# Pooled sums of the first batch on TensorE, loads of the second batch on SyncE, constants and masks later

## The chip, the cores and the metric

One core of one Trainium2 chip. The metric is the device time of one execution of the program in microseconds (us); every time below is in us from the start of the profiled span unless it says otherwise.

## The reference, cut to what matters

Inputs are q, k, v of 4 batches, 8 heads, 576 positions and 64 numbers a head, and the weights of two mixtures of experts. The first stage adds two attentions: one over queries, keys and values pooled by fours, and one over the neighbours less than four positions away.

```
q_d, k_d, v_d = (x.reshape(B, H, Sd, 4, D).mean(axis=3) for x in (q, k, v))
out_up = np.repeat(sm_attn(q_d, k_d, v_d), 4, axis=2)
out_local = softmax(where(|i - j| < 4, scale * q @ k.T, -1e9)) @ v
x = out_up + out_local                        # 2304 tokens of 512
x = x + gate * relu(x @ w1[e]) @ w2[e]        # best of 8 experts, where x @ w_skip > 0
out = sum over the two best of 8 experts of weight * relu(x @ u1[e]) @ u2[e]
```

All of it is computed in fp32 or in splits that keep its precision.

## The kernel before, in words

**Stages.** From about 1 to 130 us the attention runs, with the routing of the first mixture beside its second half; then come the experts of the first mixture and, from some 300 us on, those of the second.

**Units and pushes.** The attention is a list of units. `Local(t)` is one of 18 tiles of 128 tokens (four windows of 32), `Pooled(b, u)` is one of five parts of the pooled attention of batch b. `push(unit)` (from line 1104) writes out one step of a software pipeline: the scores of this unit (PE, then the maximum and the subtraction on DVE), the transposes (`turn`) of the unit two pushes back (`D1`), a list of fills that other code has asked for with `schedule(n, f)` (f runs n pushes later), the exponential (ACT), and `values` of the unit three pushes back (`D2`). PE, ACT, DVE and POOL keep this written order; SP's order is the planner's, which places a transfer when it expects it to be ready. In this text push n is the n-th call, from 0: pushes 0 to 3 are tiles 0 to 3, 4 to 6 are P(0,4), P(0,0), P(0,1), 7 is tile 4, 8 and 9 are P(0,2), P(0,3), 10 is tile 5, 11 to 13 are P(1,4), P(1,0), P(1,1), 14 is tile 6, 15 and 16 are P(1,2), P(1,3), 17 is tile 7; the pooled units of batch 2 begin with push 20.

**Sums of four.** A pooled unit of batch b needs qd (queries summed by fours) and kd (keys in two halves, [:, :, 0] and [:, :, 1]). For batch 0 all are reductions on DVE (`tensor_reduce`, four of qd, four of each half of kd; lines 776 and 786). For batch 1 all are additions on POOL: three for kd[:, :, 0] and three for qd (line 759), three for kd[:, :, 1] (line 789), in this order, from push 7 on. For batch 2 the queries are summed on POOL (`pool_q`, push 10). `pool_v(b, 0)` and `pool_v(b, 1)` sum the values by fours with matmuls (lines 798 and 805) and copy them out on ACT; the second then asks for the values of the next batch (`load_v`), into the same buffer. They run at push 3 for batch 0, push 7 for batch 1, push 14 for batch 2.

**Loads.** `load_qk(b)` (line 752) loads queries into qT (1152 KB) and the two halves of the keys into kT (576 KB each). For batch 1 the queries are issued by POOL, the first half of the keys by SP and the second by ACT. `load_local(t)` (line 890) loads the values of the windows of tile t in two halves of 192 KB, one issued by SP and one by ACT. An issue is an instruction in its engine's order: while it waits, what is written behind it waits too.

**POOL's order around the change.** Clears of buffers and index patterns (pushes 0 and 1), a small store to x_d, the queries of batch 1, `routing_constants` (lines 160 to 188, called by `start_3` at push 2), the four loads of `load_wall` (line 1182, at push 3), then the sums of batch 1. The masks that `start_3` asks for are two DVE operations each (lines 709 and 710). `load_wall` also asks for a copy into `wall` on DVE 12 pushes later (line 1183), which `x_part` uses. `finish(t)` schedules for each tile the addition of the pooled part (`x_add`, POOL, line 1006), its transposes on PE one push later (`x_turn`, line 1012) and the logits.

**Start.** 20 warm matmuls on zeros (`WARM`, line 621) run on PE while the first queries and keys arrive.

Of the kernel before, what the change touches and what calls it, by code (L numbers as in the profile page):

```python
# [10 lines left out]
F32 = mybir.dt.float32  # L11
# [3 lines left out]
AF = mybir.ActivationFunctionType  # L15
OP = mybir.AluOpType
# [8 lines left out]
NPOOL = S // 4  # L25
# [13 lines left out]
CH = ((0, 384), (384, 640))  # L39
EARLY = CH[0][1] // BLK2  # L40
MAGIC = 12582912.0
WARM = 20
FILL = 0
FILLS = {2: 2}
BUSY = {"turn15": 1, "table": 2, "turn16": 3, "part16": 1, "end": 3}
# [32 lines left out]
D2 = 3  # L78
NEP = 3
EPS = 48  # L80
ONDVE = (0,)
ONPOOLQ, ONPOOLQD, QDP, WALLP = (1,), (2,), 0, 12
NVG = 1
XB = 8
UB = 4
LOADQK = (-1, -1, 5, 9)
POOLQK = (2, 4, 6, 10)
POOLV = (3, 4, 6, 10)
QKS = 4
VS = 0  # L90
PATTERN = ((4, 0, 1), (2, 3))
POOLED = (3, 5, 9, 12)

# [10 lines left out]
def moe_attention_kernel(ctx, tc, q, k, v, w_skip, w_gate, w1, w2, g2, n2, noise, u1, u2, out, dbg=None):  # L104
# [507 lines left out]
    with ExitStack() as actx:  # L612
# [124 lines left out]
            load_qk(1)  # L737

        def start_3():
            routing_constants()  # L740
            for d in offsets:
                mask(d)


        fours = at.tile([128, 32], F32, name="fours", bufs=1)
# [2 lines left out]
        def load_qk(b):  # L748

            held["k", b % 2] = b  # L750
            qT[b] = at.tile([128, 4, S], F32, name="qT", bufs=2)
            (nc.gpsimd if b == 1 else nc.sync).dma_start(qT[b], q[b])
            for g in range(2):
                (nc.sync, nc.scalar)[g].dma_start(kTs[b % 2][g:128:2, g], k[b, 64 * g:64 * g + 64])

        def pooled_on_gpsimd(o, x):
            x = x.rearrange("p a (g r) -> p a g r", r=4)
# [7 lines left out]
        def pool_qk(b, n):  # L765


            assert held["k", b % 2] == b
            held["kd", b % 2] = (b, n)
            if n == 0 and b not in ONPOOLQD:  # L770
                qd[b] = at.tile([128, 4, NPOOL], F32, name="qd", bufs=2)
            kd, kT = kds[b % 2], kTs[b % 2]
            if n >= 8 and b in ONDVE:
                for i in range(n - 8, 4, 3):
                    o, x = kd[:, i, 1], kT[:, 1, i]
                    nc.vector.tensor_reduce(o, x.rearrange("p (g r) -> p g r", r=4), axis=AX.X, op=OP.add)
            elif b in ONPOOLQ and n < 8:
                if n == 0:
                    pooled_on_gpsimd(kd[:, :, 0], kT[:, 0])
                    pooled_on_gpsimd(qd[b], qT[b])  # L780
            elif n % 2 == 0 and n < 8 and b in ONPOOLQD:
                pass
            elif n < 8:
                i = n // 2
                o, x = (qd[b][:, i], qT[b][:, i]) if n % 2 == 0 else (kd[:, i, 0], kT[:, 0, i])
                nc.vector.tensor_reduce(o, x.rearrange("p (g r) -> p g r", r=4), axis=AX.X, op=OP.add)
            else:
                o, x = kd[:, :, 1], kT[:, 1].rearrange("p a (g r) -> p a g r", r=4)
                nc.gpsimd.tensor_tensor(o, x[:, :, :, 0] if n == 8 else o, x[:, :, :, n - 7], op=OP.add)
# [378 lines left out]
        pooled_keys(0)  # L1168
        pooled_keys(1)
        vgs[0] = load_v(0, A)  # L1170

        nc.vector.tensor_scalar(before, jp, 0.0, None, op0=OP.is_gt)
        nc.vector.memset(onesb, 1.0)
# [15 lines left out]
        for t in range(NT):  # L1189
            for b in range(B):  # L1190
                if LOADQK[b] == t:
                    load_qk(b)
                    if b in ONPOOLQD:
                        schedule(QDP, pool_q, b)
                if POOLQK[b] == t:
                    for n in range(8):
                        schedule(n // QKS, pool_qk, b, n)
                    for n in range(3):
                        schedule(n // 2 if b in ONDVE else n, pool_qk, b, n + 8)
                if b == 0 and t == EXP4 and UPE:  # L1200
                    schedule(0, expansion)
                if POOLV[b] == t:
                    schedule(0, pool_v, b, 0)
                    schedule(VS, pool_v, b, 1)
            if t == 3:
                load_wall()
            if t < 3:
                schedule(0, lambda: None)
# [762 lines left out]
```

## Time and profile before

| what | value |
| --- | --- |
| median of 3 runs (lowest to highest) | 780.25 us (778.61 to 781.01) |
| the profiled execution's own time | 780.45 us |
| its span, first to last instruction | 778.5 us |
| busy time of PE / DVE / ACT / POOL in the span | 755.6 / 351.3 / 249.6 / 255.0 us |
| mean granted clock of TensorE | 0.989 |

PE is TensorE's matmuls, PEld its weight loads, DVE VectorE, ACT ScalarE, POOL GpSimd, SP SyncE; a q behind an engine's name marks its issuing queue. [...] Matmuls are pipelined and their ends are modelled, so starts are surer than durations. An fp32 matmul is recorded as two passes. "idle before" names what ended the idle time of an engine; where the engine named had long been done, it was another, often a transfer.

### The profile page before, as it was taken

Reading aid. Unit: us, or ns where it says so; the run is one execution under the profiler, and the core shown is the slowest. Engines: PE = TensorE matmul, PEld = TensorE weight load, DVE = VectorE, ACT = ScalarE, POOL = GpSimd, SP = SyncE. Lnnn points to the kernel's source line nnn. Section 1 sums busy time; section 2 is a strip of 40 time slices with the busy share of each in tenths; the row PEclk is TensorE's granted clock in tenths of the full one; section 3 lists DMA queues with packets and bytes.
Section 4 is the critical chain, followed back from the end, with each engine's and each line's share of the span. In section 5 each row is a group of like instructions: output and inputs, shape, how many; then the busy total and the mean of one; then the engine's idle time right before and its main releaser. Section 6 shows DMA issues by size and latency. Waiting matters only on the chain.

```text
span 778.5 us, 15158 instructions
## 1 busy us (share of the span) xinstructions
PE 755.6 (97%) x6215; PEld 664.3 (85%) x6215; DVE 351.3 (45%) x805; ACT 249.6 (32%) x492; POOL 255.0 (33%) x257
## 2 busy tenths in 40 slices
PE   6999998999999999999999999999999999999996
PEld 3567785999999999989998998998998997997984
DVE  8776877510111755469854343262242343342200
ACT  3444553111112133224334343233233242333211
POOL 8782422211232351133364205215115115002012
PEclk9899999999999999999999999999999999999998
DMA  8988578699988872331556626526436336333013
GB/s 287 301 263 272 156 187 283 183 371 355 314 313 259 307 282 97 103 69 43 144 170 172 180 82 166 112 87 174 105 106 159 80 110 159 87 84 67 8 16 46
DMA packets 61128, 131.51 MB, mean 169 GB/s; under 512 B 15585, under 2 KB 16928, under 8 KB 59520
## 3 DMA queue, kind: packets, MB, share of 16 engines
q1 hardware_dynamic: 31552, 56.64, 23.4%
q10 hardware_dynamic: 17248, 46.66, 16.6%
q0 software_dynamic: 12256, 27.21, 16.6%
q8 instruction: 50, 0.82, 0.4%
q14 instruction: 22, 0.18, 0.1%
HBM read 101.86 MB, written 23.91 MB: 162 GB/s over the span
## 4 chain that ended last, share of the span: by engine, by line
PE 76%; issue 2%; DVE 1%; DMA 1%; POOL 0%; ACT 0%; POOLq 0%; DVEq 0%; ACTq 0%
PE pY L1612 27%; PE pH L1595 26%; PE pH L560 9%; PE pY L573 9%; PE pT L1580 2%; PE pT L592 1%; PE pT L539 1%; DMA rows<-x_d,ix2g 1%; PE pT L346 1%; PE pH L581 0%; POOL out L317 0%; DVE w L337 0%; PE pH L597 0%; PE pT L223 0%; DVE hl L1600 0%
## 5 line engine op out<-in xcount | busy, mean ns | idle before, releaser
L1612 PE MATMUL pY<-w,hh 128*128 128x512 f32 (+6 forms) x640 | 201.5, 396 | 0.0
L1595 PE MATMUL pH<-xh,w 128*128 128x256 f32 (+7 forms) x1024 | 196.0, 303 | 0.0
L1595 PEld LDWEIGHTS pH<-xh,w 128*128 128x128 f32 x1024 | 162.9, 188 | 0.8
L1612 PEld LDWEIGHTS pY<-w,hh 128*128 128x128 f32 (+6 forms) x640 | 115.0, 183 | 27.6
L1271 DVE TENSOR_TENSOR w<-stg,w 128x1024 fp32r<-128x1024 f32 x64 | 82.5, 1298 | 108.1 <-ACT w L1270 108.0
L1612 PE MATMUL pY<-w,hl 128*128 128x512 f32 (+6 forms) x320 | 125.6, 393 | 0.0
L1595 PE MATMUL pH<-xl,w 128*128 128x256 f32 (+7 forms) x512 | 123.5, 302 | 0.0
L1600 DVE SCALAR_TENSOR_TENSOR hl<-pH,hh 128x256 fp32r<-128x256 f32 (+7 forms) x128 | 57.0, 474 | 128.8 <-ACT hh L1599 128.5
L317 POOL DMA_INDIRECT out<-yo,ix2w x35 | 68.8, 1967 | 130.0 <-ACT yo L1614 121.5
L1599 ACT ACTIVATE hh<-pH 128x256 fp32r<-128x256 f32 (+7 forms) x128 | 49.3, 424 | 151.8 <-PE pH L1595 151.6
L1595 PEld LDWEIGHTS pH<-xl,w 128*128 128x128 f32 x512 | 90.1, 188 | 0.0
L312 POOL DMA_INDIRECT rows<-x_d,ix2g x32 | 36.2, 1132 | 155.4 <-PE pT L1580 144.2
L1612 PEld LDWEIGHTS pY<-w,hl 128*128 128x128 f32 (+6 forms) x320 | 58.5, 183 | 15.3
L573 PE MATMUL pY<-hT,w 128*128 128x112 f32 (+7 forms) x512 | 69.2, 296 | 0.0
L1270 ACT ACTIVATE w<-stg 128x1024 fp32r<-128x1024 f32 x64 | 66.8, 1054 | 6.8 <-DMA stg<-in_moe_w 6.8
L1614 ACT ACTIVATE yo<-pY,gt 128x512 f32<-128x512 f32 (+6 forms) x35 | 24.1, 688 | 138.3 <-PE pY L1612 77.4
L573 PEld LDWEIGHTS pY<-hT,w 128*128 128x128 f32 x512 | 67.4, 190 | 0.2
L560 PE MATMUL pH<-xT,w 128*128 128x200 f32 (+6 forms) x448 | 66.2, 301 | 0.0
L560 PEld LDWEIGHTS pH<-xT,w 128*128 128x128 f32 x448 | 61.1, 190 | 1.8 <-issue 1.7
L317 POOL DMA_INDIRECT l_d<-x,ix1w x15 | 14.3, 953 | 87.9 <-DVE x L600 87.0
L575 DVE COPY yT<-pY 128x224 f32<-128x224 f32 (+7 forms) x16 | 7.5, 471 | 73.8 <-PE pY L573 73.8
L1006 POOL TENSOR_TENSOR x<-x,up 128x512 f32<-128x512 f32 x15 | 19.3, 1291 | 42.5 <-DMA up<-od 32.6
(426 smaller groups left out, 851.4 us busy)
## 6 DMA issues: line engine op xcount, KB each, us to landing
w<-in_moe_w ACTq DMA_DIRECT2D x16, 2048.0 KB, 12.5
stg<-in_moe_w SPq DMA_DIRECT2D x64, 512.0 KB, 3.6
x_d<-x SPq DMA_DIRECT2D x18, 264.0 KB, 4.1
out<-zero ACTq DMA_DIRECT2D x3, 1536.0 KB, 7.6
up<-od SPq DMA_DIRECT2D x14, 256.0 KB, 5.1
qT<-in_q SPq DMA_DIRECT2D x3, 1152.0 KB, 5.5
vw<-in_v SPq DMA_DIRECT2D x18, 192.0 KB, 5.5
vw<-in_v ACTq DMA_DIRECT2D x18, 192.0 KB, 5.5
```

Of the source, the lines that this page charges most:

```text
L312: return nc.gpsimd.indirect_dma_start(out=dst, out_offset=None, in_=x_d[0:n + 1], in_offset=bass.IndirectOffsetOnAxis(ap=idx, axis=0))
L317: return nc.gpsimd.indirect_dma_start(out=dst, out_offset=bass.IndirectOffsetOnAxis(ap=idx, axis=0), in_=src, in_offset=None, **kw)
L560: nc.tensor.matmul(self.p[:, j], w[:, k, f * 128:(f + 1) * 128], self.xT[:, k], start=k == 0, stop=k == KD - 1)
L573: nc.tensor.matmul(p[:, j], w[:, f, d * 128:(d + 1) * 128], self.hT[:, f], start=f == 0, stop=f == KF - 1)
L1006: e.tensor_tensor(xs[t][:, 0:DM], xs[t][:, 0:DM], ups[t], op=OP.add)
L1270: nc.scalar.activation(hi[:, c], st[i], AF.Copy)
L1271: V.tensor_tensor(lo[:, c], st[i], hi[:, c].bitcast(F32), op=OP.subtract)
L1595: nc.tensor.matmul(p, w[:, k, fs], self.x[ch][n][:, k, 0:ch[1] - ch[0]], start=k == 0 and i == 0, stop=k == KD - 1 and i == 2)
L1599: nc.scalar.activation(hi, p, AF.Relu)
L1600: V.scalar_tensor_tensor(lo, p, 0.0, hi.bitcast(F32), op0=OP.max, op1=OP.subtract)
L1612: nc.tensor.matmul(p, h[:, f], w[:, f], start=f == 0 and i == 0, stop=f == KF - 1 and i == 2)
L1614: nc.scalar.activation(o, p, AF.Copy, scale=gate[0:n])
```

## The change

`ONDVE` becomes `ONPE`: for batch 0, qd and kd[:, :, 1] are summed by matmuls of the identity with every fourth column, four of them added up in PSUM for each of two tiles, and copied out by ACT; qd ahead of the first push, kd[:, :, 1] at pushes 2 and 3. kd[:, :, 0] of batch 0 stays on DVE. `WARM` goes from 20 to 14. The queries and both halves of the keys of batch 1 are issued by SP. The masks move from push 2 to push 5 and the constants to push 10. `pool_v` moves from push 3 to 5 (batch 0), from 7 to 11 (batch 1) and from 14 to 15 (batch 2); batch 3 stays. `load_wall` moves from push 3 to push 10 and its copy from push 15 to 16.

```
-WARM = 20
+WARM = 14
...
-ONDVE = (0,)
-ONPOOLQ, ONPOOLQD, QDP, WALLP = (1,), (2,), 0, 12
+ONPE = (0,)
+ONPOOLQ, ONPOOLQD, QDP, WALLT, WALLP = (1,), (2,), 0, 5, 6
...
-POOLV = (3, 4, 6, 10)
+POOLV = (3, 5, 6, 10)
 QKS = 4
-VS = 0
+VD = (2, 1, 1, 0)
...
         def start_3():
-            routing_constants()
-            for d in offsets:
-                mask(d)
+            schedule(7, routing_constants)
+            schedule(2, lambda: [mask(d) for d in offsets])
...
-            (nc.gpsimd if b == 1 else nc.sync).dma_start(qT[b], q[b])
+            nc.sync.dma_start(qT[b], q[b])
             for g in range(2):
-                (nc.sync, nc.scalar)[g].dma_start(kTs[b % 2][g:128:2, g], k[b, 64 * g:64 * g + 64])
+                (nc.sync, nc.sync if b == 1 else nc.scalar)[g].dma_start(kTs[b % 2][g:128:2, g], k[b, 64 * g:64 * g + 64])
+
+        def pooled_on_pe(o, x):
+            p = bank("pB", [128, 2, NPOOL])
+            x = x.rearrange("p a (g r) -> p a g r", r=4)
+            for i in range(2):
+                for j in range(4):
+                    nc.tensor.matmul(p[:, i], ident, x[:, i, :, j], start=j == 0, stop=j == 3)
+            nc.scalar.activation(o, p, AF.Copy)
...
-            if n == 0 and b not in ONPOOLQD:
+            if n == 0 and b not in ONPOOLQD + ONPE:
...
-            if n >= 8 and b in ONDVE:
-                for i in range(n - 8, 4, 3):
-                    o, x = kd[:, i, 1], kT[:, 1, i]
-                    nc.vector.tensor_reduce(o, x.rearrange("p (g r) -> p g r", r=4), axis=AX.X, op=OP.add)
+            if n >= 8 and b in ONPE:
+                if n != 9:
+                    pooled_on_pe(kd[:, n - 8:n - 6, 1], kT[:, 1, n - 8:n - 6])
...
-            elif n % 2 == 0 and n < 8 and b in ONPOOLQD:
+            elif n % 2 == 0 and n < 8 and b in ONPOOLQD + ONPE:
                 pass
...
         vgs[0] = load_v(0, A)
+        qd[0] = at.tile([128, 4, NPOOL], F32, name="qd", bufs=2)
+        for i in (0, 2):
+            pooled_on_pe(qd[0][:, i:i + 2], qT[0][:, i:i + 2])
...
-                        schedule(n // 2 if b in ONDVE else n, pool_qk, b, n + 8)
+                        schedule(n // 2 if b in ONPE else n, pool_qk, b, n + 8)
...
-                    schedule(0, pool_v, b, 0)
-                    schedule(VS, pool_v, b, 1)
-            if t == 3:
+                    schedule(VD[b], pool_v, b, 0)
+                    schedule(VD[b], pool_v, b, 1)
+            if t == WALLT:
                 load_wall()
```

## Rows read from the trace of the kernel before

**Rows 1.** The page: PE's busy time, clock and GB/s by slices of 19.46 us, last chain.

```profile
PE 755.6 (97%) x6215; PEld 664.3 (85%) x6215; DVE 351.3 (45%) x805; ACT 249.6 (32%) x492; POOL 255.0 (33%) x257
...
PEclk9899999999999999999999999999999999999998
...
GB/s 287 301 263 272 156 187 283 183 371 355 314 313 259 307 282 97 103 69 43 144 170 172 180 82 166 112 87 174 105 106 159 80 110 159 87 84 67 8 16 46
...
PE 76%; issue 2%; DVE 1%; DMA 1%; POOL 0%; ACT 0%; POOLq 0%; DVEq 0%; ACTq 0%
```

**Rows 2.** Windows: length, busy PE, PEld, DVE, ACT, POOL, PEclk, DMA share, GB/s.

```profile
10.00:20.00 10.00, 5.50 (x124) 3.07 (x117) 9.11 (x20) 1.60 (x4) 8.96 (x37) 0.84 1.01 285
20.00:30.00 10.00, 9.38 (x123) 5.69 (x120) 8.51 (x18) 4.30 (x10) 5.82 (x34) 0.65 1.00 333
...
40.00:50.00 10.00, 8.15 (x100) 6.38 (x99) 6.08 (x16) 3.70 (x8) 8.10 (x6) 0.83 0.79 255
```

**Rows 3.** Timeline of PE: start, duration, line, operation, count, idle before it and releaser.

```profile
1.17 7.13 PE L621 MATMUL pW<-warm 128*128 128x512 bf16 x20 [1.17 <-DVE zcol L135]
...
18.79 1.93 PE L798 MATMUL pT<-v,fours 128*32 128x512 f32 x8 [4.50 <-DMA v<-in_v]
...
33.35 1.07 PE L798 MATMUL pT<-v,fours 128*32 128x512 f32 x8 [0.18 <-DMA v<-in_v]
...
34.96 0.66 PE L866 MATMUL pB<-vd,epT 128*32 128x130 f32 x24
...
35.55 0.75 PE L829 MATMUL pA<-kd,qd 128*128 128x288 f32 x2
...
37.08 0.70 PE L829 MATMUL pA<-kd,qd 128*128 128x288 f32 x2
...
38.67 0.29 PE L951 MATMUL pA<-mask,identb 128*128 128x304 bf16 x1
...
40.04 1.08 PE L995 MATMUL pB<-vw,eT 128*32 128x128 f32 x32
42.97 0.69 PE L832 MATMUL pA<-kd,qd 128*32 128x288 f32 x8 [1.85 <-POOL kd L789]
...
49.81 0.30 PE L951 MATMUL pA<-mask,identb 128*128 128x304 bf16 x1
...
57.71 0.60 PE L1012 MATMUL pT<-ident,x 128*128 128x128 f32 x4
```

**Rows 4.** Timeline of POOL from 18 to 43 us.

```profile
18.93 0.29 POOL L160 IOTA desc<- 128x8 f32 x1
...
22.25 0.59 POOL L1182 DMA_DIRECT2D gates<-in_moe_w_gate  x1
...
28.38 1.29 POOL L759 TENSOR_TENSOR kd<-kT 128x576 f32<-128x576 f32 x1 [3.94 <-DMA kT<-in_k]
...
39.42 3.49 POOL L789 TENSOR_TENSOR kd<-kd,kT 128x576 f32<-128x576 f32 x2
```

**Rows 5.** Timeline of ACT: the issue of the second half of the keys.

```profile
18.82 0.52 ACTq L754 DMA_DIRECT2D kT<-in_k  x1
```

**Rows 6.** DMA issues from 18.5 to 19 us: KB each, us from issue to landing.

```profile
kT<-in_k ACTq DMA_DIRECT2D x1, 576.0 KB, 9.4
```

**Rows 7.** Chain of waits in order of time: start, duration, engine, count.

```profile
150.54 5.61 PE pH L560 x48
...
172.53 8.21 PE pH L560 x48
```

**Rows 8.** Groups by line and shape, PE, 0 to 160 us: busy us, mean ns.

```profile
L560 PE MATMUL pH<-xTb,w 128*128 128x112 f32 x64 | 7.9, 279 | 0.7 <-ACTq L1643 0.7
```

**Rows 9.** Timeline of DVE: the first reduction of queries of batch 0.

```profile
13.36 0.74 DVE L786 TENSOR_REDUCE qd<-qT 128x144 f32<-128x576 f32 x1
```

**Rows 10.** Timeline of all engines around 73 us.

```profile
73.13 0.52 ACTq L890 DMA_DIRECT2D vw<-in_v  x1
...
73.43 0.60 PE L995 MATMUL pB<-vw,eT 128*32 128x128 f32 x10 [0.31 <-issue]
```

## The prediction

> **What bounds the kernel now.** I read the page first [rows 1]: PE is busy for 97% of the 778.5 us, and the chain that ended last lies on PE for 76% of the span, from 150 us to the end without a hole. So nothing that this change touches can shorten the expert stages; it can only move the moment at which attention hands over to them, and what it moves there should move the end. [...] PE [rows 3] sits idle 4.50 us before 18.79, waiting for the values in pool_v(0), and later 1.85 us before 42.97, where the scores of unit P(1,4), the first pooled unit of batch 1, wait for POOL. POOL [rows 4] waits for the keys of batch 1 until 28.38 and then makes nine additions without a break up to 42.91 (39.42 + 3.49). This is the reading that decides: **the chain "keys of batch 1 land, nine additions on POOL, P(1,4)" sets PE's clock hand at 42.97**, and whatever PE gains ahead of it is given back there unless the chain itself begins earlier. I call push 11 the one that starts at 42.97 and push 14 (tile 6) the one that starts at 49.81; behind that PE goes on with small gaps only.
>
> **Where the chain begins.** What has to be read for it are the queries, keys and values of batch 0, eight halves of local values, and the queries and keys of batch 1: 4 x 1152 + 8 x 192 + 1152 KB, some 7.5 MB. The page [rows 1] moves 287 GB/s in the first slice of 19.46 us, so 5.6 MB, and 301 GB/s in the next; the remaining 1.9 MB take 6.3 us and end at 25.7. Now they end at 28.2 (issue 18.82 [rows 5] plus 9.4 to landing [rows 6]), since ACT issues the keys late and values of batch 1 pass in between. That ACT issues at 18.82 has a reason that can be read off: it is the moment at which the values land on which PE waits until 18.79, a transfer that has nothing to do with the keys, so the issue was held behind an earlier transfer's completion. With both issues on SP and the values of batch 1 asked for later (they follow pool_v(0), now two pushes later), I take 26.0. The late end is 28.2 (nothing gained, the bytes being the same); the early end is 24.4, if the two last local halves on ACT's queue (384 KB, 1.3 us at 301 GB/s) are served behind the keys. The nine additions keep their 14.5 us: push 11 starts at 40.6 (39.0 to 42.8) instead of 42.97.
>
> **When PE gets there.** WARM falls from 20 to 14, so the warm matmuls end near 7.1 instead of 8.30 [rows 3], at the full clock that the first slice shows. The sums are four calls of eight matmuls, each recorded as two passes: 64 passes of 144 columns. The chain of waits gives 5.61 us for 48 passes of 112 columns and 8.21 for 48 of 200 [rows 7]: 0.117 and 0.171 us each, so 0.13 for 144 columns, 2.1 us a call. The other end is a pass that overlaps nothing: 0.279 us [rows 8], 4.5 us a call. Pushes 0 to 10 hold six Local units (some 2.5 us each) and five pooled ones (1.53 us, from 35.55 to 37.08 [rows 3]), less 3.3 us of turns and values that follow later: 19.3 us. With pool_v(0) at 1.6 us (33.35 to 34.96), the query sums (4.2) and the key sums (4.2) PE is there at 7.1 + 4.2 + 19.3 + 1.6 + 4.2 = 36.4, and at the dear end 46.0. I take the cheap price, since 112 and 200 columns enclose 144; then PE is early by 4.2 us and all this is hidden.
>
> **What else lies ahead of push 11**, at no cost while PE is 4.2 us early, and at the price named if not: eight reductions of 0.74 us [rows 9] leave DVE and four mask operations move three pushes on (a gain of up to 5.9 us on DVE that nothing waits for); ACT gets four copies out of PSUM and loses the hold before 18.82; the wait for the values goes, and what is late next on PE is the POOL chain. If SP put the queries of batch 1 even ahead of the keys of batch 0, the first scores would wait 1152 KB longer, about 4 us at 287 GB/s, which the 4.2 us just cover.
>
> **Behind push 11.** From 42.97 to 49.81 PE needed 6.84 us. At the full clock the like of push 11 took 1.53 us (35.55 to 37.08), that of push 12, with a Local's turn, 1.59 (37.08 to 38.67), and push 13, with a Local's values (1.08 for 0.66), comes to 1.95: 5.1 in all, so 1.7 us went to the lower level that the window of 40 to 50 shows after the idle time. pool_v(1) moves from push 7 to push 11, so out of PE's slack and behind the wait: +1.6 us. The clock's part I keep at 1.7, because PE waits again (4.2 us instead of 1.85); its ends are 0 and 3.4. So push 14 starts at 40.6 + 5.1 + 1.6 + 1.7 = 49.0, **0.8 us earlier**.
>
> The constants (from 18.93) and the four gate loads (from 22.25, to 24.4 [rows 4]) lay in POOL's wait. They now stand behind the chain, 5.5 us ahead of the query sums of batch 2: POOL has those at 40.6 + 5.5 + 4.8 = 50.9, two key additions (3.0) and the first x_add (1.3) at 55.2. The first x_turn needs that at 57.71 [rows 3]: covered by 2.5 us, and 1 us lost if the keys of batch 2 come in between. The wall copy moves one push later and the gates land about 10 us after 43: no cost, at most 1 us. The values of batch 2 are asked for after pool_v(1), near 42.5, and land, if they take as long as the keys did (9.4 us [rows 6]), at 51.9; pool_v(2), one push later than before, wants them near 51: 0, at most 0.9 us.
>
> One more hold like that at 18.82 stands at 73.13: ACT's issue waits, and PE's L995 breaks in two, 0.31 us of bare idle and 0.65 us in all [rows 10]. [...] The queries of batch 1 leave POOL's software queue for a hardware one, so from there on each issue has another one ahead of it. I count the 0.65 us as won; the other end is that a new hold costs as much.
>
> **The sum**: -0.8 - 0.65 = -1.45 us on the profiled execution, which is 780.45 us (778.5 of span and 1.95 around it) and stands 0.2 above the median of 780.25: 779.0 there, **778.8 us** on the median. A measurement of this kernel can tell about 0.3% from no change, 2.3 us.
>
> **Rivals.** (A) *The keys come at 24.4* and PE waits too little to lose clock: push 11 at 39.0, push 14 at 39.0 + 5.1 + 1.6 = 45.7, -4.1 - 0.65: 775.5. For it: both issues are free of ACT's hold, and SP's transfers are the large ones. Against it: the bytes and the queues' rate are the same. (B) *The sums are dear.* Each matmul reads every fourth number of a row of keys or queries; no matmul of the kernel before does that, so no row speaks against it. At 0.279 us a pass PE comes to push 11 at 46.0, TensorE takes POOL's place as the bound, and push 14 starts at 46.0 + 6.7 = 52.7: +2.9, 783.2, slower (the hold of 73.13 not counted as won). It decides from 0.195 us a pass on, where PE is later than 40.6, and loses from about 0.23 on. (C) *The loads land no earlier* (28.2): push 11 at 42.8, push 14 at 42.8 + 8.4 = 51.2, +1.4: 781.7, and 783.4 with the doubled clock loss. For it: the DMA engines are taken to 1.00 from 10 to 30 us [rows 2].
>
> [...]
>
> **Numbers.** Forecast 0.40, (A) 0.27, (B) 0.18, (C) 0.15. The range takes in (A) with 1 us to spare, (B) and (C): 774.5 to 783.5. Faster than 777.9: most of (A) and a fifth of the forecast, 0.33. Slower than 782.6: two thirds of (B), a third of (C), 0.19. The rest, 0.48, is within 0.3%.
>
> **What would show it.** Right: no wait of PE for the values near 18; POOL's first L759 near 26 and L832 of P(1,4) near 40.6 with idle time before it that ends on POOL; L951 of tile 6 near 49; passes of the sums 0.13 us apart. Wrong: passes 0.25 us apart or more and no idle time before L832 (B); L759 still at 28 (C); a new stall at pool_v(2) on its values, at x_turn on x_add, or a hold of ACT's queue in a new place; and if push 14 is early but 150 us is not, my view that the stages behind it only shift.

## The result and the profile after

The changed kernel takes **790.24 us** (median of 6 runs, 789.26 to 792.75), the kernel before 780.11 in the 6 runs beside it (777.35 to 781.01): 1.0141 times as long, with a 95% interval of 1.0118 to 1.0164. Ratios here and below are taken from the runs themselves and differ a little from the quotients of the medians, here 1.0130. One run of kernel e7 below (793.58 us), in which the chip was in a slower state, is left out of its ratio. The forecast was 778.8 with a range of 774.5 to 783.5, so it was wrong in sign and the time lies outside the range. The profiled execution took 789.26 us with a span of 787.3, 8.8 us more than the 778.5 of before.

The page of the kernel after, same columns as [rows 1]:

```profile
PE 768.5 (98%) x6270; PEld 676.9 (86%) x6273; DVE 351.4 (45%) x797; ACT 252.7 (32%) x496; POOL 252.4 (32%) x256
...
PEclk9989999999999999999999999999999999999999
...
GB/s 303 191 248 291 189 179 253 202 294 348 324 325 256 325 294 152 110 58 26 134 162 163 225 80 151 116 82 162 102 94 179 93 108 155 76 86 75 9 13 48
...
PE 77%; issue 1%; DVE 1%; DMA 1%; POOL 0%; ACT 0%; POOLq 0%; DVEq 0%; ACTq 0%
```

The last chain is the same as before: from the hand-over on (159.37 here, the last 80% of the span) it lies on PE but for some 3%. The windows of after, columns as in [rows 2], show that the early stretch changed its character: PE is busy nearly throughout from 10 to 30 at the full clock (9.84 and 10.00 us, before 5.50 and 9.38), and the hole has moved to 30 to 50.

```profile
10.00:20.00 10.00, 9.84 (x130) 7.54 (x131) 3.75 (x8) 2.68 (x6) 7.25 (x29) 1.00 1.04 297
20.00:30.00 10.00, 10.00 (x107) 7.41 (x106) 4.16 (x9) 1.84 (x4) 3.45 (x3) 1.00 0.48 144
30.00:40.00 10.00, 8.18 (x156) 5.16 (x155) 9.58 (x13) 3.58 (x8) 9.69 (x7) 1.00 0.80 234
40.00:50.00 10.00, 9.07 (x123) 7.54 (x123) 8.11 (x22) 4.15 (x9) 9.68 (x42) 0.66 0.83 277
```

PE's timeline of after, answering to [rows 3] (L957, L838, L872 and L1018 here are L951, L832, L866 and L1012 of before; L760 is new, the sums):

```profile
1.17 5.51 PE L621 MATMUL pW<-warm 128*128 128x512 bf16 x14 [1.17 <-DVE zcol L135]
6.52 8.34 PE L760 MATMUL pB<-qT,ident 128*128 128x144 f32 x32
14.68 0.31 PE L957 MATMUL pA<-mask,identb 128*128 128x304 bf16 x1
...
18.30 4.25 PE L760 MATMUL pB<-kT,ident 128*128 128x144 f32 x16
...
23.78 4.25 PE L760 MATMUL pB<-kT,ident 128*128 128x144 f32 x16
...
36.74 0.30 PE L957 MATMUL pA<-mask,identb 128*128 128x304 bf16 x1
...
40.93 1.09 PE L872 MATMUL pB<-vd,epT 128*32 128x130 f32 x24 [2.75 <-DVE x L1006]
...
49.72 0.67 PE L838 MATMUL pA<-kd,qd 128*32 128x288 f32 x8
...
56.62 0.30 PE L957 MATMUL pA<-mask,identb 128*128 128x304 bf16 x1
...
87.19 0.66 PE L1018 MATMUL pT<-ident,x 128*128 128x128 f32 x4 [1.71 <-POOL x L1012]
```

The waits of before at 18.79 (values) and 42.97 (POOL) are both gone. In their place stand 16.4 us of sums (6.52 to 14.68, 18.30 to 22.38, 23.78 to 27.95), a wait for DVE of 2.75 us before 40.93, in which the granted clock falls to its lower level, to stay there until about 47 (0.50 from 40.25 to 46.75, 0.66 in the window of 40 to 50; before had 0.50 from 17 to 27 and from 45 to 47, in and behind its two waits), and a wait of 1.71 us for POOL's x_add before 87.19. Push 11 starts at 49.72, 8.9 us behind POOL's last addition, so POOL no longer bounds it. Compared by the start of each tile, the kernel after is 5.0 us late at tile 4 (36.74 against 31.73), 6.8 at tile 6, and 8.8 when the experts start (159.37 against 150.54).

DVE's timeline says what it did while PE waited, and POOL's what ran beside it (the first row answers to [rows 4]; the rows at 34.34 and 39.19 are each the second of two additions, the last one of the pair in the row ahead of it):

```profile
32.93 1.39 DVE L709 TENSOR_TENSOR mscr<-dj 128x38 f32<-128x38 f32 x1
34.36 1.87 DVE L710 TENSOR_SCALAR mask<-mscr 128x304 bf16<-128x304 f32 x1
36.33 1.08 DVE L709 TENSOR_TENSOR mscr<-dj 128x38 f32<-128x38 f32 x1
37.45 1.84 DVE L710 TENSOR_SCALAR mask<-mscr 128x304 bf16<-128x304 f32 x1
39.21 0.55 DVE L995 TENSOR_REDUCE sums<-e 128x8 f32<-128x392 f32 x1
```

```profile
26.40 1.21 POOL L766 TENSOR_TENSOR kd<-kT 128x576 f32<-128x576 f32 x1 [8.17 <-DMA kT<-in_k]
...
34.34 1.70 POOL L766 TENSOR_TENSOR qd<-qd,qT 128x576 f32<-128x576 f32 x1
36.01 1.35 POOL L795 TENSOR_TENSOR kd<-kT 128x576 f32<-128x576 f32 x1
...
37.43 3.44 POOL L795 TENSOR_TENSOR kd<-kd,kT 128x576 f32<-128x576 f32 x2
...
39.19 1.68 POOL L795 TENSOR_TENSOR kd<-kd,kT 128x576 f32<-128x576 f32 x1
```

The four mask operations take 6.2 us together, and they go in step with POOL: each ends (34.32, 36.23, 37.41, 39.29) within 0.25 us of the moment at which POOL passes from one addition to the next (34.34, 36.01, 37.43, 39.19).

### The profile page after: what moved, and what is told of

Read it like the earlier page. It is cut to its first block, busy times and chain, and to the rows that moved or that the text cites. A ratio compares the mean times of both kernels' runs of the same rounds, so it can differ in the third digit from the quotient of the medians.

```text
span 787.3 us, 15264 instructions
## 1 busy us (share of the span) xinstructions
PE 768.5 (98%) x6270; PEld 676.9 (86%) x6273; DVE 351.4 (45%) x797; ACT 252.7 (32%) x496; POOL 252.4 (32%) x256
## 4 chain that ended last, share of the span: by engine, by line
PE 77%; issue 1%; DVE 1%; DMA 1%; POOL 0%; ACT 0%; POOLq 0%; DVEq 0%; ACTq 0%
PE pY L1621 27%; PE pH L1604 27%; PE pH L560 9%; PE pY L573 9%; PE pT L1589 2%; PE pT L592 1%; PE pT L346 1%; PE pT L539 1%; DMA rows<-x_d,ix2g 1%; PE pH L581 0%; POOL out L317 0%; DVE w L337 0%; PE pH L597 0%; PE pT L223 0%; DVE hl L1609 0%
## 5 line engine op out<-in xcount | busy, mean ns | idle before, releaser
L560 PE MATMUL pH<-xT,w 128*128 128x200 f32 (+6 forms) x448 | 66.2, 301 | 0.0
L560 PEld LDWEIGHTS pH<-xT,w 128*128 128x128 f32 x448 | 61.1, 190 | 1.8 <-issue 1.7
L1012 POOL TENSOR_TENSOR x<-x,up 128x512 f32<-128x512 f32 x15 | 19.1, 1284 | 48.0 <-DMA up<-od 31.1
```

Source lines behind the costliest of these rows:

```text
L560: nc.tensor.matmul(self.p[:, j], w[:, k, f * 128:(f + 1) * 128], self.xT[:, k], start=k == 0, stop=k == KD - 1)
L1012: e.tensor_tensor(xs[t][:, 0:DM], xs[t][:, 0:DM], ups[t], op=OP.add)
```

## The experiments

Ratios are to the kernel before, run on the same chip in the same rounds, with the 95% interval; its median there was 779.76 us beside e1 to e4, 779.74 beside e5 to e8, 779.06 beside b1 to b4 and 781.05 beside e9, b5, c1 and c2. The starts of tiles 4, 6 and 17 and of the experts' L560 x48 (150.54 in [rows 7]) are those of one profiled execution each, and single executions scatter (last section). e10 and e11, at the end, ran once each, for their rows alone (788.31 and 788.72 us, before 782.79).

| kernel | median us | ratio | tile 4 | tile 6 | tile 17 | experts |
| --- | --- | --- | --- | --- | --- | --- |
| before | 780.11 | 1 | 31.73 | 49.81 | 113.05 | 150.54 |
| after | 790.24 | 1.0141 (1.0118 to 1.0164) | 36.74 | 56.62 | 120.42 | 159.37 |
| e1: after, masks early | 795.29 | 1.0187 (1.0151 to 1.0224) | 36.17 | 50.43 | 123.24 | 164.91 |
| e2: after, sums on DVE | 787.88 | 1.0092 (1.0060 to 1.0125) | 34.30 | 52.96 | 117.31 | 157.10 |
| e3: after, neighbouring columns | 787.18 | 1.0098 (1.0070 to 1.0126) | 31.69 | 50.44 | 113.72 | 153.80 |
| e4: e1 and e2 together | 786.06 | 1.0072 (1.0036 to 1.0108) | 34.06 | 49.48 | 115.78 | 154.84 |
| e5: e1, values of batch 1 early | 788.33 | 1.0107 (1.0066 to 1.0149) | 36.53 | 52.30 | 116.11 | 155.14 |
| e6: e4, 20 warm matmuls | 786.12 | 1.0092 (1.0056 to 1.0128) | 33.11 | 51.41 | 116.00 | 153.44 |
| e7: e4, values early, narrow loads on POOL | 783.70 | 1.0034 (1.0007 to 1.0061) | 34.93 | 49.93 | 117.12 | 155.84 |
| e8: after, values of batch 1 early | 790.26 | 1.0120 (1.0066 to 1.0175) | 37.26 | 55.17 | 121.66 | 160.78 |
| e9: after, masks and all values early | 785.26 | 1.0064 (1.0025 to 1.0103) | 36.87 | 50.92 | 113.65 | 152.22 |
| b1: before, loads on SP | 780.42 | 1.0013 (0.9988 to 1.0038) | 35.28 | 49.33 | 112.01 | 152.33 |
| b2: before, constants and gates late | 781.75 | 1.0021 (0.9998 to 1.0044) | 31.91 | 51.92 | 114.36 | 153.32 |
| b3: before, values late | 783.76 | 1.0089 (1.0045 to 1.0132) | 34.03 | 48.28 | 115.17 | 152.71 |
| b4: before, masks late | 782.65 | 1.0049 (1.0030 to 1.0067) | 31.99 | 51.35 | 112.91 | 153.47 |
| b5: before, sums on PE | 786.12 | 1.0057 (1.0034 to 1.0081) | 36.91 | 50.96 | 114.81 | 154.66 |
| c1: b1, more warm matmuls at the end | 781.34 | 1.0004 (0.9980 to 1.0028) | 33.38 | 47.43 | 111.32 | 149.89 |
| c2: before, more warm matmuls at the end | 779.93 | 0.9987 (0.9965 to 1.0010) | 30.71 | 45.10 | 108.87 | 147.57 |

### Undoing the sums and the masks

e1 makes the masks at once in `start_3`, as before:

```
-            schedule(2, lambda: [mask(d) for d in offsets])
+            for d in offsets:
+                mask(d)
```

> The changed kernel with the four mask operations back at push 2. Theory T (two separate costs: the sums on PE are dear, about 0.26 us a pass, and the masks, now beside POOL's additions, wait for them and hold DVE): the masks take 0.2 to 0.35 us each again near 20 to 25 us, PE's 2.75 us of idle time before its pooled values at 40.93 and most of the half clock behind it are gone, tile 6 starts near 52 instead of 56.62, and the time is 784 to 786.5 us. Rival R1 (the sums alone set the time; PE would stand there anyway, waiting for POOL's ninth addition): tile 6 stays near 56, 789 to 791 us. Rival R2 (the masks are the whole loss): 778 to 780 us.

The masks are short again:

```profile
19.68 0.19 DVE L709 TENSOR_TENSOR mscr<-dj 128x38 f32<-128x38 f32 x1
19.90 0.32 DVE L710 TENSOR_SCALAR mask<-mscr 128x304 bf16<-128x304 f32 x1
```

Tile 6 comes at 50.43, earlier than even theory T said (52), but the time is not shorter than after's: 1.0187 against 1.0141. PE's timeline and the windows of e1 show what came next:

```profile
57.23 1.93 PE L805 MATMUL pT<-v,fours 128*32 128x512 f32 x8 [3.76 <-DMA v<-in_v]
```

```profile
50.00:60.00 10.00, 6.24 (x97) 2.73 (x86) 6.26 (x14) 3.05 (x7) 6.16 (x5) 0.77 0.75 193
60.00:70.00 10.00, 10.00 (x140) 8.11 (x139) 5.26 (x14) 3.68 (x9) 6.00 (x5) 0.72 0.61 191
```

PE now arrives at the sums of values of batch 2 before their values do, stands for 3.76 us and then runs at the lower level of the clock until about 65.6. In the kernel after, PE was late enough by the masks not to meet this wait (e5 and e8 below test that). It does not explain by itself that e1 is slower than after: of the 6.4 us between their spans 2.8 stand at tile 17, 2.7 come between tile 17 and the experts, where the clock falls again (0.87 and 0.62 in the windows from 130 and 140), and 0.9 behind that. All three theories fall for the total; T's mechanism holds at the masks' own place.

e2 puts the sums back on DVE (eight reductions, four of queries and four of the second key halves, not twelve as its expectation has it):

```
-ONPE = (0,)
+ONPE, ONDVE = (), (0,)
...
+            elif n >= 8 and b in ONDVE:
...
+                    nc.vector.tensor_reduce(o, x.rearrange("p (g r) -> p g r", r=4), axis=AX.X, op=OP.add)
...
```

> The changed kernel with the twelve sums of batch 0 that it moved to PE back on DVE (no sums of four keys or queries on PE). Theory T: PE is no longer late at tile 4 (near 31 to 33 instead of 36.74), the masks at push 5 still run beside POOL's additions, at over 1 us each, and hold PE by some 3 us; push 11 then waits for POOL until 40.9 anyway, so that the masks' hold is mostly hidden: 778 to 782 us. Rival R1 (sums alone): 777 to 779.5 us, with nothing of the masks to be seen. Rival R2 (the masks are the whole loss): 789 to 791 us.

PE is 2.4 us earlier at tile 4 and the masks still hold it (2.45 us before 38.19), as T said. But with 1.0092 only about a third of after's loss is given back, and the two intervals just overlap; no theory's time came out.

e3 keeps the matmuls and changes the columns they read:

```
-            x = x.rearrange("p a (g r) -> p a g r", r=4)
+            x = x.rearrange("p a (r g) -> p a r g", r=4)
...
-                    nc.tensor.matmul(p[:, i], ident, x[:, i, :, j], start=j == 0, stop=j == 3)
+                    nc.tensor.matmul(p[:, i], ident, x[:, i, j], start=j == 0, stop=j == 3)
```

> The changed kernel with each of the 32 matmuls of the sums reading 144 neighbouring columns in place of every fourth one: the same number of matmuls of the same size, but it adds columns that lie 144 apart, so it does not compute the sums of four neighbours. Theory T with the stride as the cause of the price: passes 0.13 us apart instead of 0.26, first scores near 10.6 instead of 14.68, PE 8 us earlier at push 4, the masks at push 5 in part ahead of POOL's first addition at 26.4; 778 to 781 us. Rival R3 (the price is that of any 144-column fp32 pass with a weight load of its own): passes stay at 0.25 to 0.27 us, 789 to 791 us.

```profile
6.12 4.11 PE L760 MATMUL pB<-qT,ident 128*128 128x144 f32 x32
10.07 0.29 PE L957 MATMUL pA<-mask,identb 128*128 128x304 bf16 x1
```

The 32 passes last 3.95 us (to 10.07) where the kernel after needs 8.16: 0.123 us against 0.255 each. The price is that of the stride, and R3 falls. But the time is 1.0098, again only a third given back, with intervals that overlap; the masks still run beside POOL (2.99 us of idle before 36.12).

e4 is e1's edit and e2's together.

> The changed kernel with both undone: sums of batch 0 on DVE, masks at push 2. What is left of the change: WARM 14, queries and keys of batch 1 on SP, constants, gates and values later. Theory T: PE waits for POOL before push 11, POOL's chain ends near 40.9, and the forecast made without the two unforeseen costs holds: tile 6 near 49, 776 to 779.5 us. Rival R4 (something else of the change costs too, the constants behind the chain or the values late): 781 us or more.

Tile 6 stands at 49.48, where the forecast had it (49.0), yet the time is 786: R4, something else costs too. Two waits follow: 1.49 us for the values of batch 2 at 54.01 and 2.09 us for x_add on POOL before 81.31.

### The values, and what follows them

e5 has e1's edit and the sums of values of batch 1 at push 7, e8 the second alone:

```
-POOLV = (3, 5, 6, 10)
+POOLV = (3, 4, 6, 10)
...
-VD = (2, 1, 1, 0)
+VD = (2, 0, 1, 0)
```

> The changed kernel with the masks back at push 2 and the sums of values of batch 1 back at push 7 (that of batch 2 stays at push 15). Theory V (the values of batch 2 are asked for only behind the sums of values of batch 1, so that moving these from push 7 to 11, and those of batch 2 from 14 to 15 alone, leaves the load 3 pushes less; with the masks early PE runs into it): the wait of 3.76 us before the values' sums at 57.23 and the half clock behind it are gone, tile 7 starts near 57.1 instead of 64.51, and the time is 785 to 788.5 us instead of 795.3. Rival (another wait takes its place at the same spot, for the keys of batch 2 or the additions on POOL): 791 us or more.

> The changed kernel with only the sums of values of batch 1 back at push 7. Theory V with the masks' hold: in the changed kernel PE was late enough for the values of batch 2 not to be waited for, so nothing is gained: 788.5 to 791 us, and the difference to the kernel with both undone is the price of the masks alone, 2.5 to 5 us. Rival (the values cost in the changed kernel too): 786 us or less.

Both times came out as theory V said: e5 is 7 us faster than e1, with no wait near 57, and e8 is no faster than after. Between e8 and e5 the masks alone cost 2.9 us at tile 7 (61.99 against 59.12); the medians differ by 1.9 us, less than expected and well within the intervals. A smaller wait came into both, for the values of batch 1 (1.64 and 2.21 us near 40), since their load follows the sums of batch 0, still late; so tile 7 of e5 is 2 us later than V had it.

e6 is e4 with `WARM = 20`.

> The changed kernel with the sums on DVE, the masks at push 2 and 20 warm matmuls in place of 14. Theory W1 (with the sums off PE, 14 warm matmuls leave PE idle for 3.48 us before the first scores and at the lower clock from 10 to 20 us, but the sums on DVE set the pace until 24.6 us anyway): the granted clock is back near 1.00 from 10 to 16 us, tile 6 stays within 0.5 us of 49.5, 785 to 787 us. Rival W2 (that clock loss is passed on to the end): 2 to 4 us less than the 786.06 of the same kernel with 14, so 782 to 784 us.

The time is W1's: the clock is at 1.00 until 16 us, as W1 had it, where e4 has 0.50 from 12 on, and nothing of that is left at the end. Tile 6 is not W1's (51.41): push 11 waited for POOL until 42.90 (2.25 us) and the clock was at 0.83 from 40 to 50.

e7 is e4 with the values as in e5 and the narrow loads moved:

```
-                        nc.sync.dma_start(up[o, i * 128:(i + 1) * 128],
+                        nc.gpsimd.dma_start(up[o, i * 128:(i + 1) * 128],
```

> The changed kernel with the sums on DVE, the masks at push 2, the sums of values of batch 1 at push 7, and the four narrow loads of a tile's pooled part out of the or buffer issued by POOL in place of SP. Theory V: the 1.49 us wait for the values at 54 us is gone, and tile 7 starts 1.4 to 1.8 us earlier than 57.86. Theory S (in the changed kernel SP issues these four narrow loads only near 74 us, ahead of the wide loads that x_add waits for, where the kernel before issued them at 55 us; they take 2.5 us of SP's time, and so x_add is late and PE idle for 1.6 to 2.5 us before the x_turn near 81 to 88): that idle time falls to under 1 us and tile 11 starts 9.3 to 10 us behind tile 10 instead of 11.94. Both right: 781 to 783 us. Only V: 783.5 to 785. Neither: 786.

The wait at 54 is gone and tile 7 starts at 56.75, 1.1 us earlier, somewhat less than V said. PE's wait for x_add is gone too, but at the same place it idles for 1.89 us until ACT has copied the sums of values of batch 3 (at 80.63, in e4 at 78.68), the clock falls (0.66 from 80 to 90), and tile 11 is 13.4 us behind tile 10. This execution took 787.33 us, 3.6 above the kernel's median, so its rows show a bad case. The median is that of "only V". With 1.0034 it is the nearest of the partly undone versions, but not faster than before.

### Each part alone

b1 takes the two changed lines of `load_qk`, b2 the constants and `load_wall`, b3 `POOLV` and `VD`, b4 the masks, each from the diff as it stands, on the kernel before.

> The kernel before with one part of the change alone: queries and both halves of the keys of batch 1 issued by SP. Theory K1 (as in the prediction: the keys land earlier and POOL's chain ahead of push 11 with them, nothing else): first addition on POOL at 26 to 28 us, tile 6 at 47.5 to 49.8, 777 to 780 us. Rival K2 (the part that all changed kernels so far share, some 4 us more than the kernel before, comes from here: other issues of SP and ACT now wait behind these transfers, and the order of SP's later transfers is another): 782 to 785 us.

> The kernel before with one part alone: constants at push 10, gate loads at push 8 to 10 and their copy at push 16. Theory K3 (this costs nothing, as the prediction had it; POOL's constants then stand behind the additions of batch 1 and ahead of the query sums of batch 2): 778.5 to 781 us, tile 7 within 0.5 us of 56.44. Rival K4 (the sums of batch 2 and the first x_add come late on POOL): a new idle time of PE behind POOL near 55 to 60 us, 782 us or more.

> The kernel before with one part alone: sums of values at pushes 5, 11 and 15 in place of 3, 7 and 14. Theory V (one buffer holds the values, each batch's load waits for the sums of the one before, so later sums mean later loads): PE's 4.5 us wait before 18.79 goes, but push 11 waits for POOL as before (42.5 to 43), then the values of batch 2 are waited for near 54 us: tile 7 at 57.5 to 60 instead of 56.44, 781 to 784 us. Rival K5 (as the prediction had it: no cost behind push 11): 778 to 780.5 us.

> The kernel before with one part alone: the four mask operations at push 5 in place of 2. Theory M (they then run beside POOL's additions, over 1 us each, and hold DVE by 4 to 5 us; PE stands for some 2.5 us, of which its wait of 1.85 us for POOL before push 11 takes most): 780 to 782.5 us, mask operations of 1 to 1.9 us in the trace. Rival R5 (they do not wait for POOL by themselves; it was the load of the changed kernel): operations of 0.2 to 0.35 us, 779 to 780.5 us.

b1 and b2 can hardly be told from the kernel before. b1's chain does start at 26.54, as K1 had it, but nothing comes of it, since PE now waits for the values until 23.41 and starts push 10 only at 41.90, when POOL is done (40.99); its time is just above K1's range, and K2 falls. In b2 no wait behind POOL follows near 55 to 60, so K4 falls; of K3 the ratio is within its interval of no change, but the time is 0.75 us above the range and tile 7 comes at 58.54, behind a wait of 2.78 us for a chain that began at 29.30 here. b4 costs 0.49%. POOL's additions begin at 28.15 there, and three of its four mask operations are long; the first starts at 29.50, as POOL passes from one addition to the next (29.49), and is short:

```profile
29.50 0.19 DVE L709 TENSOR_TENSOR mscr<-dj 128x38 f32<-128x38 f32 x1
29.72 1.71 DVE L710 TENSOR_SCALAR mask<-mscr 128x304 bf16<-128x304 f32 x1
31.53 1.57 DVE L709 TENSOR_TENSOR mscr<-dj 128x38 f32<-128x38 f32 x1
33.14 1.31 DVE L710 TENSOR_SCALAR mask<-mscr 128x304 bf16<-128x304 f32 x1
```

PE pays for it at the next local tile's output:

```profile
36.42 0.66 PE L865 MATMUL pB<-vd,epT 128*32 128x130 f32 x24 [1.45 <-DVE x L999]
```

So R5 falls, and M's mechanism holds at its place: tile 6 is 1.5 us late. But at tile 17 this execution is level with before (112.91 against 113.05), and the 2.9 us by which its experts start late all lie behind that, where the clock falls (0.66 from 130 to 140). That the 0.49% of the medians come from the masks' hold is therefore not shown by this trace. b3 costs 0.89%, by the ratio the most, though the intervals of b3, b4 and b5 overlap. Its PE rows, and SP's of the kernel before and of b3:

```profile
53.11 1.07 PE L798 MATMUL pT<-v,fours 128*32 128x512 f32 x8 [1.79 <-DMA v<-in_v]
...
81.17 0.66 PE L1012 MATMUL pT<-ident,x 128*128 128x128 f32 x4 [2.84 <-POOL x L1006]
84.88 0.66 PE L1012 MATMUL pT<-ident,x 128*128 128x128 f32 x4 [1.10 <-POOL x L1006]
```

```profile
55.48 3.00 SPq L912 DMA_DIRECT2D up<-or  x4
...
67.81 0.58 SPq L908 DMA_DIRECT2D up<-od  x1
```

```profile
72.96 2.52 SPq L912 DMA_DIRECT2D up<-or  x4
...
75.57 1.51 SPq L908 DMA_DIRECT2D up<-od  x1
```

The values of batch 2 are waited for, as V said, but push 11 does not wait for POOL, whose chain began at 25.95 here, and tile 10 is level with before again (73.76 against 73.96). The loss follows: with the values late the planner has SP issue the four narrow loads of `up` at 72.96 instead of 55.48, and the wide load for the same tile 4 at 75.57 instead of 67.81; x_add needs both, and 2.5 of the 7.8 us are the narrow loads ahead of the wide one. All or some of the four stand that late (69 to 84) in every kernel with later sums of values (but e7, where POOL issues them) and in e9, and each of these waits for x_add of tile 4 or 5, 1.1 to 3.1 us near 81 to 89. In before, b1, b2, b4 and b5 all or three of them are issued by 61 us, and that wait is 0.87 us or less (one for ACT at this place, 1.00 or less). The distance of tile 11 from tile 10 says it most plainly: in the kernels with all sums of values at their old pushes it is 8.0 us (b4) to 9.7 (e9), 9.3 in before; in those with later ones 10.1 (e2) to 13.7 (e8), 10.3 in after and 12.2 in b3. No run moved the place of the narrow loads alone, so that their place makes the wait, and not that of the wide load, is inferred; in e7, where the wide load is back at 69.04, it is gone.

b5 is the `ONPE` part of the diff and `WARM = 14` on the kernel before. e9 is e1's edit with `POOLV = (3, 4, 6, 10)` and `VD = (0, 0, 0, 0)`.

> The kernel before with the last part of the change alone: the sums of batch 0 on PE, with 14 warm matmuls as there. Theory P (64 passes at 0.26 us are 16.7 us; PE's waits of 4.5 and 0.6 us for the values, its lower clock behind them and the 1.85 us wait for POOL take some 11 of them, 1.8 come from the warm matmuls): passes 0.26 us apart, no wait before push 11, tile 6 at 51.5 to 54 instead of 49.81, 781.5 to 784.5 us. Rival P0 (all of it is covered, and the loss of the changed kernel is the masks and the values alone): tile 6 at 49 to 50.5, 778 to 780.5 us.

> The changed kernel with the masks at push 2 and all sums of values at their old pushes 3, 7 and 14. What is left of the change: the sums on PE with 14 warm matmuls, loads on SP, constants and gates later. Theory A (the loss is made of the three parts that cost alone: sums, masks, values): no idle time of PE behind POOL's x_add near 81 to 88, tile 17 at 113.5 to 117 instead of 120.42, 780.5 to 784.5 us. Rival (the parts left cost together what none of them does alone): 786 us or more.

b5 has no wait before push 11 (45.80) and costs 0.57%, 5 us between the medians. P's passes and its missing wait hold and P0's time falls, but tile 6 comes sooner than P said (50.96, 1.2 us behind before) and the end later. Of the 4.1 us by which the experts start late in its profile, 2.4 come behind tile 17, where the clock falls (0.96 and 0.87 from 120 to 140), and PE stands 1.90 us before 65.75 for nothing that the profile shows; so where the 5 us arise is shown only in part. e9 has tile 17 only 0.6 us late and 1.0064, which is what b5, b1 and b2 cost together (0.91%) within their intervals. A holds for tile 17; its time is missed by 0.8 us (785.26, beside a before of 781.05 in those rounds), and a wait for x_add of 1.25 us is left at 83.36.

### The end of the attention, and the stride

c1 and c2 change one line, c1 on b1, c2 on the kernel before:

```
-BUSY = {"turn15": 1, "table": 2, "turn16": 3, "part16": 1, "end": 3}
+BUSY = {"turn15": 3, "table": 3, "logits15": 3, "turn16": 3, "part16": 2, "end": 5}
```

> The kernel before with the loads of batch 1 on SP (one part of the change) and eight more of the warm matmuls that the kernel places in PE's gaps at the end of the attention (near 122 to 132 us). Theory C (what makes runs of one kernel differ by several us is the granted clock in that stretch, where PE has gaps; 37.5 us from tile 17 to the experts' second turn without a drop, up to 41.7 with one): the clock stays at 1.00 from 120 to 140 us, that stretch takes 37 to 38.2 us, 776 to 778.5 us. Rival C0 (the clock falls all the same, or the added matmuls delay what they stand in front of): 779.5 us or more.

> The kernel before with only those eight more warm matmuls. Theory C: fewer of its runs lie above 780 us, median 777 to 778.8; this tells what the tail gives from what the loads give. Rival C0: 779 us or more.

These are nine more matmuls, not eight. The clock stays at 1.00 from 120 to 140, as C said, but from tile 17 to the experts it takes 38.6 and 38.7 us: the added matmuls cost some 1.1 of what the clock could give. Both times lie in C0's ranges, in rounds where the kernel before took 781.05. 4 of c2's 10 runs lie above 780 us and 17 of before's 27, fewer as C said, but neither kernel can be told from before by its ratio, so no version here beats it.

e10 and e11 read every second and every eighth column:

```
-            x = x.rearrange("p a (g r) -> p a g r", r=4)
+            x = x.rearrange("p a (h g r) -> p a h g r", h=2, r=2)
...
-                    nc.tensor.matmul(p[:, i], ident, x[:, i, :, j], start=j == 0, stop=j == 3)
+                    nc.tensor.matmul(p[:, i], ident, x[:, i, j // 2, :, j % 2], start=j == 0, stop=j == 3)
```

```
-            x = x.rearrange("p a (g r) -> p a g r", r=4)
+            x = x.rearrange("p a (g r) -> p a g r", r=8)
...
-                    nc.tensor.matmul(p[:, i], ident, x[:, i, :, j], start=j == 0, stop=j == 3)
+                    nc.tensor.matmul(p[:, i], ident, x[:, :, :, 4 * i + j], start=j == 0, stop=j == 3)
```

> The changed kernel with each matmul of the sums reading 144 columns two apart (8 bytes) in place of four apart (16 bytes): same count and size of matmuls, but it adds columns that lie further apart, so it does not compute the sums of four neighbours. [...] Rival L1 (any step over one costs): 0.2 to 0.27 us apart.

> The changed kernel with each matmul of the sums reading 144 columns eight apart (32 bytes), from both tiles of the pair, so it does not compute the sums of four neighbours. [...] Rival L2 (the price grows with the bytes stepped over): 0.4 to 0.55 us apart.

```profile
6.44 4.24 PE L760 MATMUL pB<-qT,ident 128*128 128x144 f32 x32
10.52 0.29 PE L957 MATMUL pA<-mask,identb 128*128 128x304 bf16 x1
```

```profile
6.75 8.50 PE L760 MATMUL pB<-qT,ident 128*128 128x144 f32 x32
15.08 0.31 PE L957 MATMUL pA<-mask,identb 128*128 128x304 bf16 x1
```

Per pass (to the next row's start, over 32) 0.123, 0.128, 0.255 and 0.260 us at steps of 1, 2, 4 and 8 columns: two columns cost what neighbouring ones do, eight what four do, and L1 and L2 fall.

## Why the prediction was wrong

**The sums were sized at half.** The step that failed is "I take the cheap price, since 112 and 200 columns enclose 144": the number of columns was the wrong measure to choose a row by, the step between them the right one. A pass took 0.255 us for 0.13, a call of sixteen 4.1 for 2.1. So PE was not early by 4.2 us, nothing on other engines was hidden by that, and PE took POOL's place as the bound: in e1, the changed kernel without the masks' hold, push 11 starts at 43.53 and not at 40.6, and POOL is not waited for. Rival (B) had this mechanism, with 0.279 us a pass and push 11 at 46.0. That b5 has 45.80 there is luck: b5 also has the sums of values of batch 1 ahead of push 11, 1.6 us that (B) has behind it. Nor does its 783.2 us, 0.4% above the median of before against b5's 0.57%, confirm it, since b5's profile shows only 1.2 us of its loss at tile 6 where (B) has 2.9. The sums alone did not make the loss. (B) had a chance of 0.18 where its reasons (a stride that no row showed) would have carried more. What a step costs only the runs showed: 0.123 and 0.128 us a pass at 4 and 8 bytes (e3, e10), 0.255 and 0.260 at 16 and 32 (after, e11); why it costs, none shows.

**The masks were counted at no cost.** The step is "four mask operations move three pushes on", priced at nothing because nothing waits for them. Nothing does, but DVE keeps its order, and behind them stood the sums (39.21) and the output (40.10) of a local tile that PE needed (40.93). Only who waits for the moved instruction was asked, not how long it runs in its new place. They took 6.2 us beside POOL's additions where e1's took about 1.0. This is the largest part at tile 6: with the sums on PE it comes at 55.0 to 56.6 where the masks are late (after, e8, and e11 with 54.97), and at 50.4 to 51.0 where they are early (e1, e9, b5; 52.3 in e5, which waits for values at 39.62), for a forecast of 49.0. The difference is the 2.75 us of idle time in after and the lower clock behind it (0.50): from 40.93 to tile 5 at 47.46 PE takes 6.5 us, for the same stretch in b5 3.7. Alone on the kernel before they cost 0.49% (b4). Beside the same additions other operations of DVE keep their times: the reduction of the sums takes 0.55 us at 39.21 in after as at 23.28 in before, where POOL adds nothing, and an operation that reads PSUM (line 847, 841 of before) 0.46 us at 32.56 as at 69.90 in before. Why the masks take longer there and these do not, no run shows. In before the four mask operations ran at 17.97 to 19.17 and POOL's additions from 28.38 on, so no row gave their price beside an addition, and the prediction did not ask for it.

**The values of batch 2 were sized at "0, at most 0.9 us".** The chain was described rightly: one buffer, so each load waits for the sums before it. In b3 the load is issued at 43.58 and PE gets it at 53.11, 9.5 us where 9.4 were counted. But the wait was 1.79 us, up to 3.76 where the masks did not hold PE (e1), and two things were not looked for: the clock falls behind the wait of e1 (0.77 and 0.72 in the windows from 50 and 60; behind that of b3 it stays at 1.00), and SP's order changes. With the second went 2.8 and 1.1 us of idle time in b3, and there they are what the loss at tile 17 consists of.

**What held.** POOL's chain began at 26.40 (26.0 forecast) and its nine additions took 14.5 us to 40.87. That the start came out so well is partly luck: kernels with the loads as before have it anywhere from 24.61 (c2) to 29.30 (b2), those with the new ones from 25.76 to 28.30. The constants and gates of b2 and the loads of b1 stay within their intervals of no change, while the forecast counted on 0.8 us from the loads. The hold at 73.13, counted as won with 0.65 us, is gone in after, and a wait of 0.59 us for x_add stands at 71.73. No run shows that the new order of the loads removed it: c2, with the loads of before, has no such hold, and c1, with the new ones, has one of 0.53 us at 71.22.

**The sum.** Alone, the five parts cost 0.13, 0.21, 0.89, 0.49 and 0.57%, together 2.3%; the whole change costs 1.41%. They cover each other: PE, late by the sums, no longer waits for the values; held by the masks, it does not meet the late values of batch 2. So e1, which undoes one of three losses, is not faster than after and has the highest median of all. Of the 8.8 us in the profile, tile 17 has 7.4; another 1.0 come between 134.84 and 141.21, where PE ran at the lower clock (0.83 in the window of 130 to 140) and the kernel before did not, and 0.46 behind that. The prediction held that the stages behind push 14 only shift; here they do within 2.0 us (6.8 at tile 6, 8.8 at the experts). How the median of each part comes about behind tile 17, where the clock falls in some executions (0.66 from 130 to 140 in b4) and not in others (1.00 in before and b3), stays open.

## What to carry to other kernels

A stride in the operand that TensorE streams can have its own price (fp32 here: 0.123 and 0.128 us a pass at steps of 4 and 8 bytes, 0.255 and 0.260 at 16 and 32), so look for a row with the same step, not with the same width, before choosing a price. Of a moved instruction ask three things: who waits for it, how long it will take beside what now runs on the other engines, and what stands behind it in its own engine's order. And where a load waits for the use of the batch before, moving one use later moves every load behind it; undo such parts together, since undoing one can uncover the next.

## What the runs showed of the hardware

- Landing times differed between two executions by microseconds. c2 has the same instructions in the same order as the kernel before up to its first added matmul, near 119 us; its first addition on POOL starts at 24.61 against 28.38 [rows 4], and tile 6 at 45.10 against 49.81. Of these 4.7 us only 1.1 are left in the span. So a gain of 0.8 us read from one trace in this stretch, as the prediction's was, lies inside the scatter, and so do differences of a few us between the starts in the table; verdicts here rest on several runs of each kernel.
- From tile 17 to the experts' start one profiled execution takes 37.4 to 37.5 us where the clock stays at 1.00 without added matmuls (before, b3, e6) and 38.6 to 41.7 in the kernels of the table where it falls there for some microseconds.
- From the experts' start to the end of the span it is 627.9 us (after) to 630.6 (e9), with the same instructions there: up to 2.7 us of what the attention wins or loses can go under in it.
